# One more second-order Strassen product, with its sums in the buffer of the exchanged activations

## The chip, the cores and the metric

The kernel runs on one core of one Trainium2 chip. A core has TensorE (PE in the profile; its weight loads are listed as PEld), VectorE (DVE), ScalarE (ACT), GpSimd (POOL) and SyncE (SP), which issues most of the DMAs. The metric is the device time of one execution in microseconds (us), lower is better.

## The reference

The input `x` has the shape (8, 4096, 192). A causal convolution of 7 taps runs along the sequence, with a softmaxed set of 7 weights for each of 8 heads of 24 channels; then a two-layer network with a hard-swish gate follows on 32768 tokens.

```python
w = softmax(weight, axis=-1)                       # (8 heads, 7 taps)
y = sum over k of w[head, k] * x_pad[:, t + k, :]  # (8, 4096, 192)
h = y.reshape(32768, 192) @ w_in                   # (32768, 2048)
g = h * clip(h + 3, 0, 6) / 6
out = g @ w_out                                    # (32768, 192), float32
```

## The kernel before

**Blocks.** The tokens are worked off in 32 blocks of 1024 (`TB`), each as two halves of 512 (`N`). Block 0 is handled apart, with the preparation of the weights. Blocks 1 to 31 each run `first_layer(i, jobs)` and then `second_layer(i, between)`. All instructions stand in a fixed order written by hand (`manual_schedule`): each engine works off its own list in that order, and the framework puts in the semaphores.

**First layer (line 496).** The 2048 hidden channels of both token halves are 16 groups, `n` = 0 to 15, each of two PSUM banks. `begin(n)` multiplies the high and low parts of `w_in` and `y`, ScalarE scales the sum by 4097 in place (line 520), and `end(n)` adds the mixed part; then ScalarE makes the ReLU (`relu`, line 302) and VectorE the gate (`gate`, line 306) into `g`. There are four slots of two banks; `begin(n + 4)` needs the slot that `gate(n)` frees. Groups 0 to 7 read `y_own`, groups 8 to 15 read `y_other`, the same activations with the two halves of the partitions exchanged by six DMAs (`swap_parts`, line 490, on SP's queue). In between come the `jobs`: VectorE finishes the previous block's output (`finish`), and makes taps of the convolution of the next block (line 921, one instruction for 128 x 1536 elements). After each odd group GpSimd works too: for n = 1, 3, 5, 7 four sums of 128 x 256 (`small_sums`, line 578) into the tile `s1`, and for n = 9, 11, 13 a sum of 128 x 1024 (`g_sums`, line 412) into `S3`; for n = 9 and 11 it also issues an adding DMA (line 557) that makes `S1 = A21 + A22` in place. The rest of `S1` is added by VectorE at the layer's end (line 559).

**The tiles.** `s1` and the output tile `results` share one buffer (tag "shared"), so the first write to `s1` comes after the last store DMA out of `results`.

**Second layer (line 589).** `g` is split into four quarters A11, A21, A12, A22, and the product with `w_out` is made by Strassen's seven products, P1 to P7. TensorE runs four streams side by side, each on 32 of its columns, and writes 32 PSUM partitions each. Streams 0, 1, 2 hold the three groups of 32 output columns (`q` = 0, 1, 2); stream 3 takes what is made by Strassen once more, with seven small products of half the tokens (`small`, `level_two`): two thirds of P1 and two thirds of P5. A stream has a clock in steps; a matmul on 512 tokens costs two steps, one on 256 tokens one step. Each stream comes out at 82 steps. Everything else is put between the matmuls with `do(t, ...)` at step `t - 0.5`, and the whole is sorted by step, so that `t` sets the order on each engine's list and no waiting time. Small products need sums of their operand: those of P1 are GpSimd's, those of P5 (`s5`, in A22) are made by VectorE at steps 16.2 to 34.5, and `g_sums` makes S2 and S3 from step 38 on (product 6 reads S2 from step 46 on, product 3 reads S3 from step 66 on, and both are collected in the bank `b`).

Of the kernel before, what the change touches and what calls it, by code (L numbers as in the profile page):

```python
# [25 lines left out]
def kernel(  # L26
# [16 lines left out]
    N = 512  # L43
# [76 lines left out]
    w_s = cst.tile([P, 2, 4, NP // 2, QS], F32, name="w_s")  # L120
# [375 lines left out]
    def first_layer(i, jobs):  # L496
# [44 lines left out]
        for n in range(count):  # L541
# [11 lines left out]
            if n > NP and n % 2:  # L553
                pair = slice(n - NP - 1, n - NP + 1)
                g_sums(nc.gpsimd if n + 1 < count else nc.vector, (3,), range(NP)[pair], 2)
                if n + 3 < count:
                    nc.gpsimd.dma_start(out=S1[:, pair], in_=A22[:, pair], accum_op=ALU.add)
        for pair in (slice(NP - 2, NP), slice(NP - 4, NP - 2)):
            add(S1[:, pair], A21[:, pair], A22[:, pair])
# [29 lines left out]
    def second_layer(i, between):  # L589
        last = i + 1 == NB  # L590
        ours = [free_slots.pop(0) for _ in range(3)]
        d, e, b, x_, a, c = (psum[:, 2 * n + k] for n in ours for k in range(2))
        ends = [psum[:, 2 * free_slots[0] + k] for k in range(2)] if last else [b, b]
# [6 lines left out]
        A, E = e[rows(3)], a[rows(3)]  # L600
        first, second, third, fourth = (rows(q) for q in range(4))
# [27 lines left out]
        def small(n, m_, out, start=False):  # L629

            x, w = prod[n]
            sums, ws = (s1[-1], w_s[:, 0]) if n == 1 else (s5, w_s[:, 1])
# [10 lines left out]
            for u in range(NP // 2):  # L643
                put(3, 1, lambda u=u: matmul(
                    3, out[:, lo], wm[:, u], xm[:, u], start and u == 0
# [10 lines left out]
        def tiles():  # L656
# [3 lines left out]
            late.update(zip(("p7", "p5", "u3"), (results[0][m, n] for n in range(3))))  # L660

        for q in range(NQ):
            plain(q, d, 4, q, every, True)
            before = (1, 6, NP)[q]
            plain(q, c, 7, q, every[:before], True)
            plain(q, e, 1, 2, range(5 + q, 6 + q))
            do(clock[q], copy, out=e[rows(q + 1)] if q < 2 else p1[third], in_=e[rows(q)])
            plain(q, c, 7, q, every[before:])
            plain(q, a, 2, q, every[:6], True)
            plain(q, b, 6, q, every)  # L670
            plain(q, a, 2, q, every[6:])
# [42 lines left out]
        level_two(1, lambda: p1, range(5), "1 x5 6 5 2 7 3 4")  # L714
        do(14, copy, out=e[first], in_=V)
# [7 lines left out]
        for t, n in ((16.2, 1), (16.2, 2), (30.5, 3), (34.5, 4)):  # L723
            do(t, small_sums, s5, S1, (n,), nc.vector)
        do(32, tiles)
        do(34, lambda: copy(out=late["p7"], in_=c[m]))
        do(38, copy, out=b[m], in_=p1[:])
        do(38, g_sums, nc.vector, (2,), every, 4)
        do(38, g_sums, nc.vector, (4,), every, 4)
# [289 lines left out]
```

## Time and profile before

| | before |
|---|---|
| median of 3 timed runs | 2228.0 us (2227.92 to 2228.14) |
| span of the profiled execution, first to last instruction | 2224.9 us |
| PE busy | 2218.0 us, 100% of the span |
| DVE busy | 1894.3 us, 85% |
| ACT busy | 1379.2 us, 62% |
| POOL busy | 823.8 us, 37% |
| granted TensorE clock | 0.999 |

The profiled execution has no other time on record than its span; the median of the timed runs lies 3.1 us above it, which is what lies around the first and the last instruction. Durations in the profile are those of one execution. Matmuls overlap on TensorE, so a PE that is busy for 100% is not at its peak; the start-to-start distance of its instructions tells more.

### The profile page before, as it was taken

To read this page: it belongs to the slowest core of one execution; us is meant where nothing else is said; L and a number is where in the kernel's file an instruction comes from. 1 tells how busy PE (TensorE), PEld (TensorE's weight loads), DVE (VectorE), ACT (ScalarE), POOL (GpSimd) and SP (SyncE) were. 2 spreads that over 40 slices of the span, in tenths; PEclk is the share of its full clock that TensorE was granted. 3 is DMA by queue.
4 is the path that set the end of the run, shared out by engine and by line. 5 is a ranking of instruction groups with operands and counts; after the bars stand their busy time and mean duration, and the time that the engine had idled before them with its cause. 6 is when DMAs were issued, how large, how long until landed. Compare 5 with 4: busy or idle time off the path is not lost.

```text
span 2224.9 us, 50339 instructions
## 1 busy us (share of the span) xinstructions
PE 2218.0 (100%) x21496; PEld 1532.7 (69%) x21496; DVE 1894.3 (85%) x1673; ACT 1379.2 (62%) x1678; POOL 823.8 (37%) x690
## 2 busy tenths in 40 slices
PE   9999999999999999999999999999999999999999
PEld 5467776677766777766777667776677776677766
DVE  8888888888888888888888888888888888888876
ACT  7457665576655676555766557665567655576654
POOL 2344432344422444223443234442244422344323
PEclk9999999999999999999999999999999999999999
DMA  6244224443244342344422444324434234442232
GB/s 157 57 98 85 49 58 91 85 83 62 53 82 91 77 80 47 71 91 84 85 48 58 91 87 81 67 49 82 91 79 81 47 67 91 84 84 52 55 77 34
DMA packets 253584, 166.57 MB, mean 75 GB/s; under 512 B 208017, under 2 KB 213137, under 8 KB 253361
## 3 DMA queue, kind: packets, MB, share of 16 engines
q1 hardware_dynamic: 234872, 129.46, 28.4%
q0 software_dynamic: 17248, 33.64, 8.7%
q8 instruction: 168, 2.75, 0.5%
q14 instruction: 56, 0.45, 0.1%
q10 hardware_dynamic: 1240, 0.27, 0.1%
HBM read 31.72 MB, written 25.17 MB: 26 GB/s over the span
## 4 chain that ended last, share of the span: by engine, by line
PE 99%; DVE 0%; DMA 0%; ACTq 0%; issue 0%; DVEq 0%; ACT 0%
PE psum L615 49%; PE psum L508 46%; PE psum L296 2%; PE psum L341 2%; DMA x<-in_x_dram 0%; DVE y L255 0%; DVE top L175 0%; ACTq L89 0%; PE psum L816 0%; DVE results L456 0%; DVE scale L171 0%; DVE y L251 0%; DVE scale L192 0%; DVEq L1014 0%; DVE results L462 0%
## 5 line engine op out<-in xcount | busy, mean ns | idle before, releaser
L615 PE MATMUL psum<-g,w_out 128*32 128x512 f32 (+1 forms) x6712 | 967.5, 552 | 0.0
L306 DVE SCALAR_TENSOR_TENSOR g<-g,psum 128x1024 f32<-128x1024 f32 (+1 forms) x528 | 618.3, 1186 | 198.8 <-ACT g L302 194.5
L578 POOL TENSOR_TENSOR s<-g 128x256 f32<-128x256 f32 x248 | 273.6, 1103 | 1241.1 <-DVE g L306 1200.5
L302 ACT ACTIVATE g<-psum,half 128x1024 f32<-128x1024 f32 (+1 forms) x528 | 564.8, 1087 | 6.0 <-PE psum L508 5.2
L615 PEld LDWEIGHTS psum<-g,w_out 128*32 128x32 f32 x6712 | 371.8, 110 | 246.0 <-issue 126.7
L508 PE MATMUL psum<-y,w_in 64*128 64x512 f32 x4464 | 521.4, 388 | 0.0
L508 PE MATMUL psum<-y_other,w_in 64*128 64x512 f32 x4464 | 516.0, 386 | 0.0
L520 ACT ACTIVATE psum<-psum 128x1024 f32<-128x1024 f32 x465 | 469.0, 1008 | 50.7 <-PE psum L508 48.4
L508 PEld LDWEIGHTS psum<-y,w_in 64*128 64x128 f32 x4464 | 413.5, 184 | 115.7 <-issue 26.0
L508 PEld LDWEIGHTS psum<-y_other,w_in 64*128 64x128 f32 x4464 | 418.1, 184 | 87.8
L615 PE MATMUL psum<-s,w_out 128*32 128x512 f32 (+1 forms) x3272 | 465.5, 570 | 0.0
L921 DVE SCALAR_TENSOR_TENSOR y<-x,c_sb,y 128x1536 f32<-128x1536 f32 x186 | 335.2, 1802 | 2.6 <-ACT y L919 1.3
L412 POOL TENSOR_TENSOR s<-g 128x1024 f32<-128x1024 f32 x93 | 285.9, 3074 | 26.2 <-DVE g L306 26.2
L615 PE MATMUL psum<-g,w_s 128*32 128x256 f32 x1240 | 282.8, 379 | 0.0
L615 PEld LDWEIGHTS psum<-s,w_out 128*32 128x32 f32 x3272 | 154.3, 110 | 81.9 <-issue 49.4
L615 PEld LDWEIGHTS psum<-g,w_s 128*32 128x32 f32 x1240 | 136.4, 110 | 67.7
L412 DVE TENSOR_TENSOR s<-g 128x2048 f32<-128x2048 f32 (+1 forms) x93 | 181.3, 1977 | 1.1
L615 PE MATMUL psum<-s,w_s 128*32 128x256 f32 x744 | 170.7, 379 | 0.0
L578 DVE TENSOR_TENSOR g<-g 128x1024 f32<-128x1024 f32 x124 | 151.7, 1224 | 5.3
L412 DVE TENSOR_TENSOR g<-g 128x2048 f32<-128x2048 f32 x62 | 139.1, 2284 | 0.0
L612 ACT COPY psum<-psum 32x512 f32<-32x512 f32 x93 | 51.3, 551 | 135.4 <-PE psum L615 135.4
L456 DVE TENSOR_TENSOR results<-psum,results 32x256 f32<-32x256 f32 (+3 forms) x128 | 69.3, 541 | 50.9 <-issue 45.5
(91 smaller groups left out, 1299.5 us busy)
## 6 DMA issues: line engine op xcount, KB each, us to landing
y_other<-y SPq DMA_DIRECT2D x186, 384.0 KB, 5.1
g<-g POOLq DMA_DIRECT2D x62, 512.0 KB, 5.0
out_dram<-results SPq DMA_DIRECT2D x378, 64.0 KB, 2.0
x<-in_x_dram SPq DMA_DIRECT2D x53, 388.5 KB, 7.7
stage<-in_moe_w_in_dram SPq DMA_DIRECT2D x16, 192.0 KB, 4.5
stage<-in_moe_w_out_dram SPq DMA_DIRECT2D x8, 384.0 KB, 6.8
x<-in_x_dram SPq DMA_DIRECT2D x7, 384.0 KB, 8.4
x<-in_x_dram POOLq DMA_DIRECT2D x2, 388.5 KB, 5.4
```

What stands on the lines that cost most here:

```text
L296: nc.tensor.matmul(out=psum[:, b], lhsT=w[r], rhs=src, start=start, stop=stop, skip_group_check=onto,)
L302: nc.scalar.activation(r6, h, ACT.Relu, bias=half[:], scale=1.0 / 6.0)
L306: nc.vector.scalar_tensor_tensor(out=g_, in0=g_, scalar=1.0, in1=h, op0=ALU.min, op1=ALU.mult)
L341: lambda p=p: nc.tensor.matmul(out=bank[j * QS : (j + 1) * QS, tokens], lhsT=w_out[:, p, w, cols], rhs=x[:, p, tokens], start=(first and p ...
L412: engine.tensor_tensor(out=o[:, r], in0=a[:, r], in1=b[:, r], op=op)
L456: nc.vector.tensor_tensor(out=out, in0=x, in1=y, op=op)
L508: nc.tensor.matmul(out=psum[:, 2 * slots[n] + k], lhsT=r32(w_in_parts[part][r, c, s]), rhs=r32(y_other[0][r, part, s] if group else y_own[ ...
L520: nc.scalar.mul(both(n), both(n), 4097.0)
L578: engine.tensor_tensor(out=o, in0=p, in1=q, op=op)
L612: streams[3].append((t - 0.5, lambda: fn(*args, **kw)))
L615: nc.tensor.matmul(out=out, lhsT=w, rhs=x, start=start, stop=True, tile_position=(0, j * QS), skip_group_check=True,)
L921: jobs.append(lambda k=k: nc.vector.scalar_tensor_tensor(out=y[:], in0=x[:, :, k : k + N], scalar=c_sb[:, k : k + 1], in1=y[:], op0=ALU.mu ...
```

## The change

- P2's first two thirds (`q` = 0, 1) are made by Strassen once more, too: seven small products on streams 0 and 1 in place of 16 matmuls on 512 tokens. P1's remaining third is cut into half matmuls over all four streams. Every stream then comes out at 81 steps in place of 82.
- The four sums of A12 that P2's small products need (`sums2`) are made by VectorE at the start of the second layer. They stand, with `p1`, in a new tile `z2` with the tag of `y_other`, hence in the same buffer; a third set of small weights is made once, in block 0's stage.
- Since `z2` occupies that buffer until P2 is added up (step 65.6), `swap_parts` moves from step 18 to step 70.
- All four parts of `S1` are added by DMA from GpSimd's queue; VectorE's two additions of 128 x 1024 go. Two of the four s5 sums move behind S2, to step 40, and the sums for S3 are cut in two.
- The convolution's taps are cut into three instructions of 128 x 512 each. None stands in the second layer any more; 18 of them, instead of four taps of 128 x 1536, stand in the first layer: four behind `finish`, and then 1, 2, 1, 2, 1, 2, 1, 1, 1, 1, 1 after groups 0 to 10.
- P2 is collected in `late["p2"]` by four copies and three additions on 32 or 96 partitions.

```diff
-    w_s = cst.tile([P, 2, 4, NP // 2, QS], F32, name="w_s")
+    w_s = cst.tile([P, 3, 4, NP // 2, QS], F32, name="w_s")
...
                 g_sums(nc.gpsimd if n + 1 < count else nc.vector, (3,), range(NP)[pair], 2)
-                if n + 3 < count:
-                    nc.gpsimd.dma_start(out=S1[:, pair], in_=A22[:, pair], accum_op=ALU.add)
-        for pair in (slice(NP - 2, NP), slice(NP - 4, NP - 2)):
-            add(S1[:, pair], A21[:, pair], A22[:, pair])
+                nc.gpsimd.dma_start(out=S1[:, pair], in_=A22[:, pair], accum_op=ALU.add)
...
+        z = pools[0].tile([P, NP + 1, N], F32, name="z2", tag="other")
+        sums2, p1 = z[:, 0:NP], z[0:DH, NP]
...
+        A2, B2, C2, E2 = a[rows(0)], a[rows(1)], x_[rows(0)], x_[rows(1)]
...
+        def by_half(j, bank, n, q, ch, t, start=False):
+            x, w = prod[n]
+            put(j, 1, lambda: matmul(
+                j, bank[rows(j), halves[t]], w_out[:, ch, w, q * QS : (q + 1) * QS],
+                x[:, ch, halves[t]], start,
+            ))
...
+        def after(j, fn, *args, **kw):
+            do(clock[j], fn, *args, **kw)
...
         for q in range(NQ):
             plain(q, d, 4, q, every, True)
-            before = (1, 6, NP)[q]
+            before = (0, 2, 6)[q]
             plain(q, c, 7, q, every[:before], True)
-            plain(q, e, 1, 2, range(5 + q, 6 + q))
-            do(clock[q], copy, out=e[rows(q + 1)] if q < 2 else p1[third], in_=e[rows(q)])
-            plain(q, c, 7, q, every[before:])
-            plain(q, a, 2, q, every[:6], True)
+            if q == 0:
+                by_half(0, e, 1, 2, 7, 0)
+            elif q == 1:
+                by_half(1, e, 1, 2, 4, 1)
+                plain(1, e, 1, 2, (5, 6))
+            else:
+                by_half(2, e, 1, 2, 7, 1)
+            after(q, copy, out=e[rows(q + 1)] if q < 2 else p1[third], in_=e[rows(q)])
+            if q == 0:
+                small(2, 1, A2, True, 0)
+                after(0, copy, out=B2[:, lo], in_=A2[:, lo])
+            elif q == 1:
+                small(2, 6, B2, False, 1)
+                after(1, copy, out=C2[:, lo], in_=B2[:, lo])
+            plain(q, c, 7, q, every[before:], before == 0)
+            if q == 0:
+                small(2, 7, C2, False, 0)
+                small(2, 2, A2, False, 0)
...
+            elif q == 1:
+                small(2, 5, E2, True, 1)
...
+            else:
+                plain(2, a, 2, 2, every[:6], True)
+            assert clock[q] == 45
             plain(q, b, 6, q, every)
-            plain(q, a, 2, q, every[6:])
+            if q == 0:
+                small(2, 4, C2, False, 0)
+            elif q == 1:
+                small(2, 3, B2, False, 1)
+            else:
+                plain(2, a, 2, 2, every[6:])
...
-        for t, n in ((16.2, 1), (16.2, 2), (30.5, 3), (34.5, 4)):
-            do(t, small_sums, s5, S1, (n,), nc.vector)
...
+        do(0, small_sums, sums2, A12, (1, 2, 3, 4), nc.vector)
+        do(26, small_sums, s5, S1, (1, 2), nc.vector)
...
         do(38, g_sums, nc.vector, (2,), every, 4)
-        do(38, g_sums, nc.vector, (4,), every, 4)
-        do(62, lambda: add(late["u3"], b[m], late["p7"]))
+        do(40, small_sums, s5, S1, (3, 4), nc.vector)
+        do(41.2, lambda: copy(out=late["p7"], in_=c[m]))
+        do(46, g_sums, nc.vector, (4,), range(0, 4), 4)
+        do(61.2, lambda: add(late["u3"], b[m], late["p7"]))
+        do(61.4, g_sums, nc.vector, (4,), range(4, 8), 4)
...
+        do(65.6, lambda: add(late["p2"], late["p2"], p1))
+        do(65.6, lambda: store(i, late["p2"], 0, 0))
...
-        def conv_jobs(i):
+        def conv_jobs(i, width=1):
...
             for k in range(1, KC):
...
+                for s in range(0, K3, width):
+                    jobs.append(lambda k=k, s=s: tap(k, slice(s, s + width)))
...
-            jobs = {4 * n + 1: [job] for n, job in enumerate(conv[4:])}
-            jobs[-1] = left + conv[3:4]
+            jobs = {-1: left + conv[:4]}
+            pieces = conv[4:]
+            for n, k in enumerate((1, 2, 1, 2, 1, 2, 1, 1, 1, 1, 1)):
+                jobs[n], pieces = pieces[:k], pieces[k:]
...
-                between = [(13, split_high), (15, split_rest), (18, swap_parts)]
+                between = [(13, split_high), (15, split_rest), (70, swap_parts)]
             if i + 2 < NB:
-                between += [(20, begin_conv), (60, lambda: conv[0]()), (72, lambda: conv[1]()), (73, lambda: conv[2]())]
+                between += [(20, begin_conv), (60, lambda: conv.pop(0)())]
```

## The prediction

> **What bounds the kernel now.** First the page's chain of waits, then the chain in order of time, then a table of the two stages of one block (1057.14 to 1090.05 us first layer, 1090.05 to 1125.51 second).
>
> ```profile
> PE 99%; DVE 0%; DMA 0%; ACTq 0%; issue 0%; DVEq 0%; ACT 0%
> PE psum L615 49%; PE psum L508 46%; PE psum L296 2%; PE psum L341 2%; DMA x<-in_x_dram 0%; DVE y L255 0%; DVE top L175 0%; ACTq L89 0%; PE psum L816 0%; DVE results L456 0%; DVE scale L171 0%; DVE y L251 0%; DVE scale L192 0%; DVEq L1014 0%; DVE results L462 0%
> ```
>
> ```profile
> 1057.14 32.90 PE psum L508 x288
> 1090.05 35.47 PE psum L615 x216
> ```
>
> ```profile
> core 0: us, PE busy (x) PEld busy (x) DVE busy (x) ACT busy (x) POOL busy (x), PEclk, DMA share, GB/s
> 1057.14:1090.05 32.91, 32.91 (x293) 26.84 (x296) 25.94 (x23) 30.83 (x32) 21.99 (x19) 1.00 0.16 26
> 1090.05:1125.51 35.46, 35.46 (x386) 21.15 (x386) 33.09 (x27) 11.82 (x20) 3.67 (x2) 1.00 0.59 120
> ```
>
> TensorE is the chain, at full clock: a block takes 68.37 us, and 31 such blocks are 2119 of the 2225 us. Nothing that the change does to another engine can gain time; it can only make TensorE wait. So I need how near the others are to that: VectorE has 7.0 us free in the first layer and 2.4 in the second. Its list at a block's start, and GpSimd's beside it:
>
> ```profile
> 1057.79 0.69 DVE L456 TENSOR_TENSOR results<-results 96x512 f32<-96x512 f32 x1 [1.11 <-ACT results L772]
> ...
> 1060.47 1.77 DVE L921 SCALAR_TENSOR_TENSOR y<-x,c_sb,y 128x1536 f32<-128x1536 f32 x1
> 1062.38 1.22 DVE L306 SCALAR_TENSOR_TENSOR g<-g,psum 128x1024 f32<-128x1024 f32 x1
> 1064.32 1.22 DVE L306 SCALAR_TENSOR_TENSOR g<-g,psum 128x1024 f32<-128x1024 f32 x1 [0.72 <-ACT g L302]
> 1065.46 1.81 DVE L921 SCALAR_TENSOR_TENSOR y<-x,c_sb,y 128x1536 f32<-128x1536 f32 x1
> 1067.19 2.39 DVE L306 SCALAR_TENSOR_TENSOR g<-g,psum 128x1024 f32<-128x1024 f32 x2
> 1070.39 1.22 DVE L306 SCALAR_TENSOR_TENSOR g<-g,psum 128x1024 f32<-128x1024 f32 x1 [0.82 <-ACT g L302]
> ```
>
> ```profile
> 1065.62 2.25 POOL L578 TENSOR_TENSOR s<-g 128x256 f32<-128x256 f32 x1 [40.32 <-DVE g L306]
> 1067.95 0.75 POOL L578 TENSOR_TENSOR s<-s,g 128x256 f32<-128x256 f32 x1
> 1068.65 0.74 POOL L578 TENSOR_TENSOR s<-g 128x256 f32<-128x256 f32 x1
> ```
>
> Gates come every 2.04 us. GpSimd's first sum takes 2.25 us in place of 0.74: it started inside the tap of 1065.46 and ended 0.6 after it, so a tap holds GpSimd up. The reverse, from block 0's stage:
>
> ```profile
> 9.01 2.46 DVE L255 SCALAR_TENSOR_TENSOR y<-x,c_sb,y 128x256 f32<-128x256 f32 x6
> 17.24 3.20 DVE L255 SCALAR_TENSOR_TENSOR y<-x,c_sb,y 128x256 f32<-128x256 f32 x6
> ```
>
> ```profile
> 16.86 1.32 POOL L200 TENSOR_TENSOR w_in<-sig,scale 128x384 f32<-128x384 f32 x1 [3.21 <-DVE sig L196]
> ```
>
> The same six taps take 0.74 more when GpSimd runs a sum as they start. Gates (one operand in PSUM) show no such loss at 1068 to 1072.
>
> **The change part by part.**
>
> *TensorE's steps.* 82 steps take 35.47 us, 0.4326 each; one step less is -0.43 a block. 16 matmuls on 512 tokens become 28 on 256, each of two passes: 24 passes more. Start to start, a round of four passes takes 0.4293 and one of five 0.4317, so 24 x 0.0024 = +0.06. Together -0.37, in 31 blocks **-11.5 us**. The streams now stand half a matmul apart in steps 13 to 29; the trace has no such rounds. Bounds: nothing, or an uncovered weight load (0.11, PEld row) in 16 rounds, 1.8 a block; I take nothing, by the rounds of five. The Trainium skill (TensorEngine Tiling (Array Packing), Instruction Overhead) gives every matmul some 60 cycles of overhead; as an estimate, 25 ns at the full clock, 24 passes would cost 0.6 a block and the step's gain would be gone. The rounds of five speak against it: their fifth pass cost 2.4 ns.
>
> *Taps in the first layer.* Start to start a tap of 256 elements takes 0.396 us and one of 1536 takes 1.73, so one of 512 takes 0.66. `finish` ends at 1060.47 as before. Four taps: gate 0 starts at 1063.12 in place of 1062.38, 0.74 late. A gate takes 1.14 to the next instruction, so gate and one tap 1.80, gate and two taps 2.46, against 2.04. Lateness of gates 0 to 6: 0.74, 0.60, 1.03, 0.83, 1.25, 1.01, 1.43; after that it falls by 0.24 a gate. The slack: `begin(8)` needs gate 4, which ends naturally at 1071.61; 138 matmuls of 32.90 / 288 us stand before `begin(8)`, which puts it at 1072.90, and its weights load one pair (0.23) ahead: 1.06 less the semaphore, say 1.04. So TensorE waits 1.43 - 1.04 = **0.39** a block.
>
> *GpSimd against these taps.* `s1` waits for the last store out of `results`. SP issues in order, and the exchange now stands ahead of the six stores of `finish`. VectorE's list from step 61 on (p5 0.44, u3 0.72, half of S3 2.20, p7 0.72 and 0.64, two adds 0.88, P2 0.72 and 0.64) ends 1.4 us before the layer does; then three stores at 0.5; so the exchange starts at the layer's end. It moves 2.36 MB; at the 220 GB/s of its busy slices that is 10.7 us, with the 2 of latency 12.7; the stores land behind it at about 15 us into the first layer. GpSimd starts there, where it started at 8.5, and has no pause left. From then on its 0.7-us sums stand in a row while 8 taps come: where the two take turns, the tap behind gate 4 waits for half a sum (0.3), and between the two behind gate 5 a whole one gets in (0.45 net). That is at gate 6, the latest one, so it counts in full: **0.75**. Bounds: 0 (GpSimd yields), and 1.9 (each tap waits).
>
> *The second layer.* P2's sums cost VectorE 4.7 us (four of 1.14 to 1.32) before S2; the two adds for S1 (2.28) and two s5 sums (2.4) go or move behind it. From gate 15's end to S2's first half: 15.6 before (1093.4 to 1109.0), 15.6 after, but wanted at step 45, one earlier: 0.5 of slack becomes 0.1. GpSimd's remaining work, 16 x 0.70 + 8 x 0.5 of waiting + three sums of 2.45 and two DMA issues of 1.0, ends at 15 + 24.6 = 39.6 us, while VectorE wants to start its own 128 x 1024 sum at about 37.5; before, that sum already waited 0.5. So S2 comes 0 to 2.0 late and with it product 6; I take **1.0**. The adding DMAs for the last parts of S1 are issued by about 42 and need 5.0 (page); VectorE reads S1 first at 47 or later, so they just hide, and if they don't, S2 pays for it one for one. Six more small copies on ScalarE (0.34 to 0.58 each) fall into its 23.6 us of idle time. Queued on SP behind the moved exchange are only `finish`'s stores, counted above; the load of `x` goes ahead of it.
>
> *Sum.* 30 x (0.39 + 0.75 + 1.0) = 64.2 (the last block has no taps), less 11.5: +53. On the profile: 2224.9 + 53 = 2278, and with the 3.1 around it **2281 us**.
>
> **Rivals.**
> *The step comes through* (faster): all lateness stays within the slack. VectorE has 7.0 us free in the first layer, and the taps add only 18 x 0.66 - 4 x 1.77 = 4.8. It decides if gate 6 is under 1.04 late: taps 0.06 shorter would do, if GpSimd cost nothing as well. 2228 - 11.5 = 2216. Against: the taps stand at the front, and the 7 us lie at the end too. Chance 0.17.
> *GpSimd yields*: only the late gates count: 30 x 0.39 - 11.5, 2228. Chance 0.08.
> *More collisions*: every tap waits (1.9) and the three 2.45-us sums hold VectorE's sums for the full 2.0: 30 x 4.3 - 11.5 = 117, 2345; from 2320 on I count it here. Chance 0.10.
> *The exchange comes too late*: `begin(8)` reads it 15.7 us into the layer; I have it landed at 12.7. If it takes over 3 us longer (a landing of 8.2 in place of 5.1 is the longest seen), the rest is a wait: 2 us would give 31 x 2, 2343 in all. Chance 0.03.
> *The passes' overhead* (that page's rule): +0.6 a block from odd rounds, 31 x 0.6 = 19 more, 2300. Against: the 2.4 ns. Chance 0.02.
>
> **How the numbers follow.** The forecast has 0.60. Its own range is 2245 to 2320. The range 2222 to 2330 leaves out the first rival and the far end of the third. Faster by over 0.2% (4.5 us, about what a measurement can tell here) is the first rival, 0.17; within, the second, 0.08; slower, the rest, 0.75.
>
> **What would show it.** Right: L508's stretch grows from 32.9 to about 34, with weight loads waiting for gates near groups 8 to 10; taps longer than 0.75 beside GpSimd's sums; the first sum into `s` waiting for a store and starting near 15 us; L615's stretch at 36 in place of 35.1, with a wait for S2. Wrong: a first layer of 32.9, or taps of 0.74 throughout.

## The result and the profile after

| | before | after |
|---|---|---|
| median of the timed runs | 2228.0 us (2227.91 to 2228.22) | 2545.1 us (2543.3 to 2556.4) |
| span of the profiled execution | 2224.9 us | 2542.6 us |
| granted TensorE clock, mean | 0.999 | 0.978 |
| first layer / second layer, mean of the blocks | 32.91 / 35.47 us | 33.65 / 45.19 us |

The change makes the kernel slower by 317 us: the ratio is 1.1435, 95% interval 1.1418 to 1.1452. I had forecast 2281. The sign was right; the size was far outside the range. The layers' lengths are worked out from the trace, from the first matmul of one layer to the first of the next.

The chain of waits of the page, by engine and by line, was TensorE for 99% before. Now:

```profile
PE 37%; DVE 24%; POOL 18%; DMA 8%; issue 7%; ACT 3%; SPq 2%; DVEq 0%; POOLq 0%; ACTq 0%
PE psum L615 29%; POOL s L575 12%; PE psum L508 8%; DVE y L973 8%; DMA g<-g 6%; POOL s L412 6%; DVE g L306 6%; DVE results L456 4%; DVE s L412 3%; DMA out_dram<-results 2%; SPq L372 2%; DVE g L575 2%; ACT g L302 1%; POOL g L556 1%; DVE y L9
```

One block's first and second layer, in the table of stretches:

```profile
core 0: us, PE busy (x) PEld busy (x) DVE busy (x) ACT busy (x) POOL busy (x), PEclk, DMA share, GB/s
1121.53:1155.43 33.90, 33.50 (x290) 26.55 (x289) 31.37 (x37) 30.77 (x32) 18.22 (x19) 1.00 0.48 101
1155.43:1198.15 42.72, 39.02 (x414) 19.05 (x412) 34.57 (x30) 14.24 (x26) 8.83 (x6) 1.00 0.36 61
```

In the second layer TensorE is idle for 3.7 us and busy for 39.0, where 35.1 was wanted: after a wait the four streams are out of step, and for some 4.3 us only one or two of them run (an estimate from the starts of the matmuls, with 0.43 us for one on 512 tokens and 0.21 for one on 256). How a block comes to that, as the chain in order of time tells it (start, length, what; 1121.53 is the block's start):

```profile
1131.41 0.96 SPq L372
1132.42 3.79 DMA out_dram<-results
...
1136.60 0.74 POOL s L575
...
1159.59 2.87 POOL s L412
...
1162.78 0.70 POOL g L556
1163.48 7.12 DMA g<-g
1170.72 1.24 DVE g L575
...
1173.31 0.44 DVE z L456
1173.79 3.65 PE psum L615 x26
```

The last store of `finish` is behind the exchange and lands 14.7 us into the block; GpSimd starts then, ends at 41, issues the last adding DMA, and this lands at 49.1. VectorE's first two s5 sums (L575, two of 1.2) start then, and P1's additions (L456) stand behind them. But VectorE had waited only 0.28 for the landing: its own list had come to these sums just before, at 48.9. In the whole execution its idle time ahead of them comes to 21.7 us put down to this DMA, 0.7 a block:

```profile
L575 DVE TENSOR_TENSOR g<-g 128x1024 f32<-128x1024 f32 x124 | 148.9, 1222 | 25.0 <-DMA g<-g 21.7
```

So two chains arrive together, GpSimd's with its DMA and VectorE's own list, and the chain of waits shows only the one that comes last. P1's last small product cannot start until its bank has been read: TensorE's wait there is 2.98 us. Waits of TensorE are given from the start of the last matmul ahead of the wait to the start of the next one; the time for which the profile calls it idle is some 0.4 to 0.6 shorter. Two more follow, 0.81 (step 41, behind a copy into the same bank) and 1.47 (step 67, behind the addition of P7 and P4, which stands on VectorE behind half of S3).

Why GpSimd is late, and VectorE too, is in the two lists. First GpSimd's (start, length), then VectorE's:

```profile
1145.53 0.74 POOL L575 TENSOR_TENSOR s<-s,g 128x256 f32<-128x256 f32 x1
1146.23 1.19 POOL L575 TENSOR_TENSOR s<-g 128x256 f32<-128x256 f32 x1
...
1159.59 2.87 POOL L412 TENSOR_TENSOR s<-g 128x1024 f32<-128x1024 f32 x1
```

```profile
1145.90 0.91 DVE L973 SCALAR_TENSOR_TENSOR y<-x,c_sb,y 128x512 f32<-128x512 f32 x1
1146.74 1.21 DVE L306 SCALAR_TENSOR_TENSOR g<-g,psum 128x1024 f32<-128x1024 f32 x1
...
1158.91 1.22 DVE L412 TENSOR_TENSOR s<-g 128x1024 f32<-128x1024 f32 x1
1160.06 3.50 DVE L575 TENSOR_TENSOR z<-g 128x1024 f32<-128x1024 f32 x1
...
1168.67 1.75 DVE L477 SCALAR_TENSOR_TENSOR y<-y,y 128x1536 fp32r<-128x1536 f32 x1
...
1170.72 2.56 DVE L575 TENSOR_TENSOR g<-g 128x1024 f32<-128x1024 f32 x2 [0.28 <-DMA g<-g]
1173.31 0.98 DVE L456 TENSOR_TENSOR z<-psum,z 32x256 f32<-32x256 f32 x2
```

A tap that falls into GpSimd's sums makes one of them 1.19 long in place of 0.74, while the tap itself, start to next start, takes 0.84 in place of 0.67. And VectorE's first sum for P2 starts at 1160.06, 0.47 after the start of a GpSimd sum that ends at 1162.46: if it waits for that end, its 3.50 are 2.40 of waiting and its own 1.1. From the sum behind gate 15 (1158.91) to P1's addition (1173.31) VectorE takes 14.4 us, against 9.9 in the kernel before: four sums for P2, some 4.5 by themselves, stand where two additions for S1 took 2.3, and the rest is almost all that waiting.

About half of the blocks are worse than this one (second layers of 46 to 48 in place of 42 to 44), and the first layer tells them apart. In 14 blocks VectorE gives way, as here: its taps lose about 1.1 us in all, the first layer takes 33.9 and the second 42.4 to 44.1. In 15 blocks GpSimd gives way: the taps keep their pace, five of GpSimd's sums of 128 x 256 take 1.7 to 2.5, the first layer takes only 33.3, and the second 46.1 to 48.1. The first block (40.4) stands apart. The two kinds differ in when GpSimd's first sum starts: at 14.8 to 15.2 us of the block where VectorE gives way, at 14.1 to 14.7 (once 15.5) where GpSimd does. Whether that decides it was not tested.

In the next block, one of the second kind, VectorE takes 17.9 us from the sum behind gate 15 to P1's addition, of which it waits 1.0 for the DMA. The wait at step 33 is 5.68 us, and the clock is cut (the same table, slices of 1 us around that wait):

```profile
1250.00:1251.00 1.00, 0.00 (x0) 0.00 (x0) 0.72 (x1) 0.00 (x0) 0.00 (x0) 1.00 0.00 0
1251.00:1252.00 1.00, 0.00 (x0) 0.00 (x0) 0.90 (x2) 0.00 (x0) 0.00 (x0) 0.64 0.00 0
...
1254.00:1255.00 1.00, 1.00 (x9) 0.35 (x2) 0.00 (x0) 0.00 (x0) 0.00 (x0) 0.50 0.00 0
...
1258.00:1259.00 1.00, 1.00 (x12) 0.50 (x6) 1.00 (x1) 0.00 (x0) 0.00 (x0) 0.95 0.00 0
```

TensorE's last matmul ended at 1248.3 and the next began at 1253.35. The granted clock (the number behind the bracket of POOL) halves 3.0 us into this silence and stays at 0.50 until 1258.1, 4.8 us after the work has begun again. From there to the wait at step 41 TensorE takes 6.4 us, and 4.1 in the block above, which had no cut: so the cut costs 2.3 on top of the wait. The length of a silence alone does not decide it. Of the 29 silences of over 1.5 us in this trace, from the end of one matmul to the start of the next, the two of 2.4 us left the clock alone, five of the eleven of 2.8 to 2.9 were followed by a cut, and so were all sixteen of 3.3 to 5.8. Each cut lasted 3.4 or 6.8 us, began 2.2 to 4.9 us after the last matmul, and ended 2.7 to 6.0 us after work had begun again. All in all 88 us of such work ran at half clock, which is worth at most 44 of the 317 us (an estimate from the trace's clock records). The Trainium skill (TensorE: Matmul & The Clock Gate, Part 1) says that the clock is halved after some 3.4 us without work and given back after as much sustained work. The trace agrees in size only: here a silence of 2.8 us can be enough.

### The profile page after: what moved, and what is told of

Its sections match the earlier page's. It is cut to its first block, busy times and chain, and to the rows that moved or that the text cites. A ratio compares the mean times of both kernels' runs of the same rounds, so it can differ in the third digit from the quotient of the medians.

```text
span 2542.6 us, 53029 instructions
## 1 busy us (share of the span) xinstructions
PE 2366.6 (93%) x22364; PEld 1486.7 (58%) x22364; DVE 2149.4 (85%) x2157; ACT 1452.9 (57%) x1864; POOL 918.7 (36%) x756
## 3 DMA queue, kind: packets, MB, share of 16 engines
q0 software_dynamic: 34112, 66.14, 15.2%
## 4 chain that ended last, share of the span: by engine, by line
PE 37%; DVE 24%; POOL 18%; DMA 8%; issue 7%; ACT 3%; SPq 2%; DVEq 0%; POOLq 0%; ACTq 0%
PE psum L615 29%; POOL s L575 12%; PE psum L508 8%; DVE y L973 8%; DMA g<-g 6%; POOL s L412 6%; DVE g L306 6%; DVE results L456 4%; DVE s L412 3%; DMA out_dram<-results 2%; SPq L372 2%; DVE g L575 2%; ACT g L302 1%; POOL g L556 1%; DVE y L993 1%
## 5 line engine op out<-in xcount | busy, mean ns | idle before, releaser
L615 PE MATMUL psum<-g,w_out 128*32 128x512 f32 (+1 forms) x6340 | 1058.3, 536 | 0.2 <-ACT psum L612 0.2
L575 POOL TENSOR_TENSOR s<-g 128x256 f32<-128x256 f32 x248 | 268.6, 1083 | 1473.8 <-DVE y L973 736.9
L615 PE MATMUL psum<-s,w_out 128*32 128x512 f32 (+1 forms) x3272 | 631.2, 592 | 0.0
L615 PE MATMUL psum<-g,w_s 128*32 128x256 f32 x1488 | 350.9, 406 | 141.3 <-DVE z L456 116.6
L973 DVE SCALAR_TENSOR_TENSOR y<-x,c_sb,y 128x512 f32<-128x512 f32 (+1 forms) x546 | 416.9, 790 | 1.5 <-ACT y L971 1.4
L412 POOL TENSOR_TENSOR s<-g 128x1024 f32<-128x1024 f32 x93 | 251.0, 2699 | 2.8 <-DVE g L306 2.7
L412 DVE TENSOR_TENSOR s<-g 128x2048 f32<-128x2048 f32 (+1 forms) x93 | 248.7, 2674 | 2.0
L615 PE MATMUL psum<-z,w_s 128*32 128x256 f32 x744 | 203.2, 422 | 20.7 <-ACT psum L738 13.4
L615 PEld LDWEIGHTS psum<-s,w_out 128*32 128x32 f32 x3272 | 175.9, 110 | 52.0 <-ACT psum L612 7.1
L612 ACT COPY psum<-psum 32x256 f32<-32x256 f32 x186 | 82.7, 445 | 212.4 <-PE psum L615 209.5
L456 DVE TENSOR_TENSOR results<-psum,results 32x256 f32<-32x256 f32 (+1 forms) x190 | 96.1, 506 | 115.3 <-PE psum L615 99.6
L575 DVE TENSOR_TENSOR g<-g 128x1024 f32<-128x1024 f32 x124 | 148.9, 1222 | 25.0 <-DMA g<-g 21.7
```

What stands on the lines that cost most here:

```text
L412: engine.tensor_tensor(out=o[:, r], in0=a[:, r], in1=b[:, r], op=op)
L456: nc.vector.tensor_tensor(out=out, in0=x, in1=y, op=op)
L575: engine.tensor_tensor(out=o, in0=p, in1=q, op=op)
L612: streams[3].append((t - 0.5, lambda: fn(*args, **kw)))
L615: nc.tensor.matmul(out=out, lhsT=w, rhs=x, start=start, stop=True, tile_position=(0, j * QS), skip_group_check=True,)
L973: nc.vector.scalar_tensor_tensor(out=y[:, r], in0=x[:, r, k : k + N], scalar=c_sb[:, k : k + 1], in1=y[:, r], op0=ALU.mult, op1=ALU.add,)
```

## The experiments

Three theories. **G**: GpSimd is held up by the short taps and starts late, and what it owes comes late. **V**: VectorE's list of the second layer has the wrong order, and what TensorE needs stands behind what waits. **D**: the landing of S1's last part by DMA is the loss, however the rest is arranged. The layers' lengths are means of the blocks. Where no interval is given, a kernel was run once; the five executions of the changed kernel lie within 13 us of each other, those of the kernel before and of the last one within 2.

| kernel | first / second layer | us | against before |
|---|---|---|---|
| before | 32.91 / 35.47 | 2227 | |
| + short taps | 33.27 / 37.70 | 2305 | +78 |
| + exchange at step 70 | 33.07 / 36.32 | 2257 | +30 |
| + S1 all by DMA | 32.92 / 48.64 | 2624 | +397 |
| + S1 by DMA, exchange | 33.02 / 38.95 | 2337 | +110 |
| + all three | 33.29 / 43.92 | 2493 | +265 |
| after (P2 on top) | 33.65 / 45.19 | 2545 | +317 |

Where S1 is all by DMA, the first two s5 sums stand at step 26, as in the change (16.2 before).

**Parts of the change, each put into the kernel before.** The taps:

```diff
-            jobs = {4 * n + 1: [job] for n, job in enumerate(conv[4:])}
-            jobs[-1] = left + conv[3:4]
+            jobs = {-1: left + conv[:4]}
...
+            for n, k in enumerate((1, 2, 1, 2, 1, 2, 1, 1, 1, 1, 1)):
```

> The kernel before with only the convolution's taps cut into 128 x 512 and moved into the first layer, as in the change. Theory G (GpSimd falls behind in the first layer, by the late start of its sums and by taking turns with VectorE's taps, and hands S1 over late): L508's stretch grows by 0.4 us (gates late) plus 0.3 to 0.8 (collisions), L615's stays within 0.5 of 35.47, so 2228 + 30 x 0.7 to 1.5 = 2249 to 2273 us. Theory V (the waits come from the order of VectorE's list in the second layer, which stands unchanged here): only the late gates count, 2228 to 2242 us.

Measured 2305, beyond both theories. The first layer grows by 0.36 (0.28 in most blocks), the second by 2.2, though not one instruction of it was changed. GpSimd's list and VectorE's, then VectorE's list of the kernel before at the same place:

```profile
1059.86 2.86 POOL L412 TENSOR_TENSOR s<-g 128x1024 f32<-128x1024 f32 x1
```

```profile
1057.77 2.13 DVE L412 TENSOR_TENSOR s<-g 128x1024 f32<-128x1024 f32 x1
1059.94 5.01 DVE L456 TENSOR_TENSOR g<-g 128x1024 f32<-128x1024 f32 x2
...
1070.80 0.43 DVE L456 TENSOR_TENSOR p<-psum,p 32x256 f32<-32x256 f32 x1
```

```profile
1093.45 1.71 DVE L412 TENSOR_TENSOR s<-g 128x1024 f32<-128x1024 f32 x1
...
1103.39 0.43 DVE L456 TENSOR_TENSOR p<-psum,p 32x256 f32<-32x256 f32 x1
```

From the sum after gate 15 to P1's addition VectorE took 9.9 us before, with no idle time between, and TensorE had no wait for the addition: the matmul behind it began 0.84 after its end. Now GpSimd's last sum runs in the same place, the same stretch takes 13.0, and TensorE waits 1.94 for P1's addition. So of 3.1 us 0.8 were slack, and the rest is the second layer's growth. G and V are two halves of one thing: GpSimd's lateness reaches TensorE through VectorE's list, here without any adding DMA on the way.

The exchange:

```diff
-                between = [(13, split_high), (15, split_rest), (18, swap_parts)]
+                between = [(13, split_high), (15, split_rest), (70, swap_parts)]
```

> The kernel before with only the exchange of y moved from step 18 to step 70. Theory G: the stores of finish land some 7 us later, GpSimd's first sum starts near 14 us into the first layer in place of 8.5, its last 128 x 1024 sum ends some 4 us later and VectorE's own sum and additions at the layer's end wait for it: 1 to 2.5 us a block, 2259 to 2305 us. Theory V: GpSimd may start late but nothing in the chain waits for it, 2228 to 2235 us.

Measured 2257, just under G's range: GpSimd's first sum starts at 13.5 us of the block in place of 8.5, its last ends at 38.7 (36.9).

S1 all by adding DMA:

```diff
-                if n + 3 < count:
-                    nc.gpsimd.dma_start(out=S1[:, pair], in_=A22[:, pair], accum_op=ALU.add)
-        for pair in (slice(NP - 2, NP), slice(NP - 4, NP - 2)):
-            add(S1[:, pair], A21[:, pair], A22[:, pair])
+                nc.gpsimd.dma_start(out=S1[:, pair], in_=A22[:, pair], accum_op=ALU.add)
```

> The kernel before with one part of the change: all four pairs of S1 added by DMA, and the s5 sums 1 and 2 at step 26 as in the change (16.2 before). Nothing else is altered: 82 steps, whole taps, the exchange at step 18. Theory D: GpSimd's last sum ends at 36.9 us of the block, the DMA is issued by 39 and lands 7 to 8 later, 13 to 14 us into the second layer, where step 26 is at 11.2: the s5 sums wait 2 to 3 us with P1's additions behind them, TensorE loses 1 to 3 us a block, time 2260 to 2320. Theory V: here VectorE has no sums for P2, is freed of two additions (2.3 us), and nothing is lost: 2224 to 2240.

Measured 2624, worse than the whole change, and far beyond both theories. The chain in order of time, and the table of stretches over the wait:

```profile
1277.78 17.34 DMA g<-g
...
1298.31 23.07 PE psum L612 x125
```

```profile
1287.00:1298.30 11.30, 0.99 (x10) 0.08 (x3) 2.89 (x4) 1.16 (x2) 0.00 (x0) 0.75 0.91 197
1298.30:1321.00 22.70, 22.69 (x218) 11.64 (x218) 19.50 (x16) 4.32 (x8) 0.00 (x0) 0.90 0.12 19
```

The adding DMA takes 17.3 us where the changed kernel's takes 7.1, because the exchange goes out at step 18 just as it is issued: the DMA engines are busy for 0.91 of the wait. VectorE waits 14.8 us for it, TensorE 10.9 behind VectorE, and then it runs at a mean clock of 0.90.

Both together (S1 as above, exchange at 70):

> The kernel before with two parts of the change together: S1 all by adding DMA (s5 sums 1 and 2 at step 26, as in the change) and the exchange at step 70. With S1 by DMA alone the last adding DMA, issued as the exchange runs, took 17.3 us to land and the time was 2624; with the exchange at 70 alone it was 2257. Theory D' (an adding DMA and the exchange in flight together hold each other up, so the two parts belong together): the landing falls to 7 to 8.4, the s5 sums wait 2 to 4 us past their place, time 2290 to 2370. Theory D (the adding DMA is slow by itself): 2500 or more.

Measured 2337, as D' has it; the last adding DMA of the block at 963.77 landed in 6.6 us. So the two edits belong together: moving the exchange costs 30 by itself and saves 287 once S1 is added by DMA. All three, without P2's second level:

> The kernel before (82 steps, P2 plain) with the change's three other parts together: taps cut and moved, the exchange at step 70, S1 all by adding DMA with s5 1 and 2 at step 26. Without the taps' part it was 2337. Theory G (short taps hold GpSimd up, and every microsecond of that goes through the adding DMA into the s5 sums): 2420 to 2490, and P2's second level with its four sums and its list accounts for the remaining 55 to 125 of the change's time. Theory V (most of the loss is P2's own, VectorE's list): 2345 to 2375, and P2 accounts for 170 or more.

Measured 2493: G, 3 us above its range. 265 of the change's 317 us come with the three edits that touch no TensorE step. The other 52 are not simply the price of P2's second level. In this kernel VectorE stands idle for 146 us in all, 4.9 a block, for the adding DMA; in the change P2's four sums fill most of that time (21.7 us are left). And here GpSimd gives way in 25 of 30 blocks, in the change in 15. Among blocks of the same kind P2 adds 2.5 us to the second layer where GpSimd gives way (44.9 to 47.4) and 3.8 where VectorE does (39.3 to 43.1).

**Parts of the change undone.** S1's last two pairs by VectorE again:

```diff
+                if n + 3 < count:
...
+        for pair in (slice(NP - 2, NP), slice(NP - 4, NP - 2)):
+            add(S1[:, pair], A21[:, pair], A22[:, pair])
```

> The changed kernel with the last two pairs of S1 added by VectorE at the end of the first layer, as in the kernel before; all else as changed. Theory D (S1's last landing by DMA, 7 to 8.4 us behind GpSimd's end, holds the s5 sums): the landing is gone, the s5 sums start 2.5 to 3.5 us earlier, time 2435 to 2470. Theory V (VectorE is too full at the layer's start): the two additions (2.3 to 5 us beside GpSimd) now stand ahead of the four sums for P2, TensorE waits for these at step 13 or so, and the gain is eaten: 2510 or more.

Measured 2597 (33.58 / 47.02), 52 worse than the change, as V has it. The edit takes the landing away but puts two additions onto VectorE ahead of P1's, so it does not by itself measure what the landing costs; that D is not the sole cause rests on VectorE's 0.7 a block above and on the taps alone, which lose without it. Without the landing, VectorE's own list is the chain (the chain in order of time of one block):

```profile
1183.51 4.31 DVE s L412
...
1188.98 1.22 DVE g L456
...
1200.71 0.44 DVE z L456
1201.19 5.00 PE psum L618 x26
```

The taps whole and at their old places:

> The changed kernel with the taps whole (1536 elements) and where they were in the kernel before; all else as changed. Theory G (GpSimd loses its turns to the short taps, ends at 41 to 44 us of the block in place of 37, and the last adding DMA and the s5 sums with it come 2 to 6 us later): the L615 stretch falls by 3 to 5 us, time 2390 to 2450. Theory V (the order of VectorE's list decides, whenever GpSimd ends): only the first layer gains its 0.7, 2520 to 2530.

Measured 2463 (33.06 / 43.06), 82 better, between the two theories. The second layer falls by 2.1, less than G says, to what the better half of the changed kernel's blocks have: the last adding DMA still takes 7.2 behind GpSimd's end, and VectorE's first sum for P2 still meets a GpSimd sum (4.07).

The exchange from GpSimd's queue in place of SP's:

```diff
-        nc.sync.dma_start(out=to[D2:P], in_=part[0:D2])
+        dma.dma_start(out=to[D2:P], in_=part[0:D2])
```

> The changed kernel with the exchange issued from GpSimd's queue in place of SP's, so that the stores of finish don't stand behind it. Theory G: GpSimd's first sum starts near 9 us into the first layer in place of 14 to 15, the last adding DMA lands some 5 us earlier, and a block loses 4 to 5 of its 10 us of waits: 2390 to 2430 us. Theory V: VectorE still waits in the same places, 2480 us or more.

Measured 2582, in V's range, but it decides nothing, since what the edit was to bring did not come: SP's stores no longer stand behind the exchange in a queue, but they are still late (GpSimd's first sum at 13.7 us), and GpSimd has six issues more.

**The order of VectorE's list.** Only the places at which the s5 sums and the addition of P7 and P4 stand:

```diff
-        do(26, small_sums, s5, S1, (1, 2), nc.vector)
+        do(29.2, small_sums, s5, S1, (1, 2), nc.vector)
...
-        do(62, lambda: add(late["p7"], late["u3"], d[m]))
+        do(61.3, lambda: add(late["p7"], late["u3"], d[m]))
```

> The changed kernel with two moves in VectorE's list alone: the first two s5 sums go from step 26 to 29.2, behind the first addition to p1, and P7's second addition from step 62 to 61.3, ahead of the second half of S3. Theory V: the wait of TensorE before step 33 (3.0 us in one block) and the one before P5's fourth small product (1.5 us) go, 2545 - 31 x 4 = 2420 us or less. Theory G: S1 still comes late, and product 6 waits for S2 in place of step 33; only the 1.5 us go, 2480 to 2510 us.

Measured 2470 (33.39 / 42.93), 75 better and just better than G's range; V's 2420 is not reached. With the sums at 33.2, behind both of P1's additions:

> The changed kernel with two places of its list altered, no work more or less: the s5 sums 1 and 2 stand at step 33.2 (26 in the change), behind both additions of P1 in place of ahead of them, and the addition of P7 and P4 at 61.3 (62). Theory V (what TensorE loses in the second layer, it loses to additions that stand on VectorE behind the s5 sums, which wait for the adding DMA): both of P1's additions now run before the wait, the L615 stretch falls from 45.2 to 38 or less, time at most 2330. Theory D (the late landing itself is the loss, because S2 and product 6 stand behind the s5 sums wherever these are put): the wait only moves, to product 6 or the second group of P5; L615 at 41 or more, time 2415 or more. With the s5 sums at 29.2, between the two additions, it was 2470 and 42.9.

Measured 2471 (33.38 / 42.96), where theory D put it, but not for D's reason. The adding DMA is gone from the chain (VectorE's idle time for it is 5.3 us in all), but the list before it is not shorter: gate 15, a sum of 4.45 and one of 3.98 beside GpSimd, three more for P2, the two operations that split y. TensorE's gaps only move (1.97 at step 24, 2.10 at 33, 2.23 at 49). Then the whole list in due order (the lines that these replace, and the two halves of `split_rest` as functions, are left out):

```diff
-                between = [(13, split_high), (15, split_rest), (70, swap_parts)]
+                between = [(13, split_high), (24, split_low), (29.1, split_mix), (70, swap_parts)]
...
+        do(33.2, small_sums, s5, S1, (1,), nc.vector)
+        do(38, g_sums, nc.vector, (2,), range(0, 4), 4)
+        do(38.1, small_sums, s5, S1, (2,), nc.vector)
+        do(38.2, g_sums, nc.vector, (2,), range(4, 8), 4)
+        do(45.6, small_sums, s5, S1, (3, 4), nc.vector)
```

> The changed kernel with VectorE's list of the second layer put in the order in which TensorE wants its parts, no work more or less: the split of the next block's y (two operations of 1.75) goes from step 15 to 24 and 29.1, each behind what is due before it; the s5 sums at 33.2, 38.1 and 45.6, between them the halves of S2; the addition of P7 and P4 at 61.3. Theory V (order): VectorE is then never behind by itself, the L615 stretch falls below 38, time 2320 or less. Theory G (VectorE is late because its own first sums run beside GpSimd's 2.4 to 2.9 us sums and take 4 in place of 1.2, and because GpSimd ends late): the list still starts some 5 us late, the stretch is 39.5 to 41.5, time 2370 to 2430.

Measured 2394 (33.40 / 40.46): G, so order alone does not do it. Upon that, whole taps (one at step 74, one ahead of gate 0, one behind each of gates 1, 3, 5, 7):

> As the run before (list in due order), and the taps whole: one at step 74, one ahead of gate 0, and one behind each of gates 1, 3, 5 and 7. Theory G: GpSimd, no longer cut off by short taps, ends 2 to 3 us earlier, but its last sum still runs beside VectorE's first ones: the stretch is 37 to 39.5, time 2290 to 2370. Theory V: no more than the first layer's 0.5, within 20 us of the run before.

Measured 2312 (33.14 / 37.98): G again. Upon that, the sum behind gate 13 on VectorE:

```diff
+                if n + 3 == count:
+                    held = pair
+                    continue
+                for pair in ([held] if n + 1 == count else []) + [pair]:
```

> As the run before (due order, whole taps), and the sum into S3 behind gate 13 made by VectorE behind gate 15 in place of GpSimd, so that GpSimd has done when VectorE's own sums start. Theory G: the sums take 1.2 again, the last adding DMA is issued some 3 us earlier, VectorE meets every step, and the 81 steps come through: L615 35.1 to 36, L508 33.0, time 2215 to 2250. Theory D (the landing of S1's last part holds the s5 sums however early it is issued): the stretch stays above 37, time 2290 or more.

Measured 2295 (33.13 / 37.42), which is D's range, but VectorE's idle time for the adding DMA is 0.6 us in the whole execution. VectorE's first sums take no more than 1.58 now, but the steps do not come through: the trace shows no wait of TensorE over 0.81 us in the block, and 2.3 us lost in small ones.

**Whether small waits add up.** Four of those waits mended by moving single operations:

```diff
-                    do(clock[3], steps[k])
+                    do(45.1 if (n, k) == (5, 1) else clock[3], steps[k])
...
-        do(38.2, g_sums, nc.vector, (2,), range(4, 8), 4)
+        do(45.1, g_sums, nc.vector, (2,), range(4, 8), 4)
...
-        do(61.2, lambda: add(late["u3"], b[m], late["p7"]))
+        do(60.9, lambda: add(late["u3"], b[m], late["p7"]))
...
-                between = [(13, split_high), (24, split_low), (29.1, split_mix), (70, swap_parts)]
+                between = [(4.6, split_high), (24, split_low), (29.1, split_mix), (70, swap_parts)]
```

> The kernel of c3_n13 with the four waits mended that its trace still shows, no work more or less: the copy of A to B in P5 goes from step 41 to 45.1 (TensorE's start of P2's fifth part stood 0.81 behind it, same bank), P2's addition ahead of the second half of S2 (0.4 at step 49), the addition of U3 ahead of P5's addition (0.8 at step 65, of which half), and the split on ScalarE from 13 to 4.6 (0.27 at step 20). Theory of single waits (they add up): L615 falls from 37.4 by 1.9 to about 35.5, time 2230 to 2242. Theory of a further bound (VectorE's list as a whole is the limit): the waits move, 36.5 or more, 2265 or more.

Measured 2304 (33.25 / 37.62), a miss: the moved copy now stands right ahead of P5's second part, which needs it, and TensorE waits 1.64 there in place of 0.81. The other three are smaller or gone. The exchange early (with c5_waits as the start):

```diff
-        do(61.4, g_sums, nc.vector, (4,), range(4, 8), 4)
...
+        do(65.6, g_sums, nc.vector, (4,), range(4, 8), 4)
...
+                between = [(4.6, split_high), (24, split_low), (29.1, split_mix), (65.7, swap_parts)]
```

> As c5_waits, and P2 ended ahead of the second half of S4, so that the exchange goes out some 4 us earlier (step 65.7, ahead of P2's stores). Theory G: s1 starts 3 to 5 us earlier, GpSimd ends earlier, the last landing too; what is left of the late sums goes, 2222 to 2235. Rival: with an earlier start GpSimd meets one or two more whole taps, the first layer grows by 0.3 to 0.6, and nothing waits for GpSimd's end any more: 2238 to 2255.

Measured 2341 (33.39 / 38.60), above both: the second half of S3, now behind P2's additions, is 1.37 late for product 3, which neither theory had. One more chunk of P5 between the copy and its reader, again from c5_waits:

```diff
-            "1 l4 2 6 5 7 3 l2 4 l2 h8" if last else "1 x2 2 6 5 7 3 x1 4 x5",
+            "1 l4 2 6 5 7 3 l2 4 l2 h8" if last else "1 x3 2 6 5 7 3 4 x5",
```

> As c5_waits, with one more chunk of P5 between its first and second part (three in place of two), so that the moved copy of A has two steps before A is written again. Theory of single waits: the 1.64 at step 45 goes, L615 35.7 to 36.1, time 2240 to 2255. Theory of a further bound: 37 or more, 2280 or more.

Measured 2361 (33.39 / 39.36), in the range of a further bound. The wait ahead of P5's second part fell to 0.79, but the later parts of P5 now meet reads of their banks: 1.52 at step 61 and 0.81 at step 65. And P1 in another order, with one copy out of its bank later:

```diff
-        level_two(1, lambda: p1, (), "6 5 2 7 3 4")
+        level_two(1, lambda: p1, (), "6 5 7 3 2 4")
...
-            after(q, copy, out=e[rows(q + 1)] if q < 2 else p1[third], in_=e[rows(q)])
+            do(clock[q] if q < 2 else 33.1, copy, out=e[rows(q + 1)] if q < 2 else p1[third], in_=e[rows(q)])
```

> As c7_order5, and in P1 the parts in the order 6 5 7 3 2 4 (6 5 2 7 3 4), so that part 3 no longer starts behind a copy into its bank (0.4 at step 29). Theory of single waits: L615 35.2 to 35.7; with a first layer of 33.2 this is 68.6 a block against 68.4 before, time 2224 to 2242: no gain is left, since what the step saves (0.37) goes into gates that are late behind the taps (0.3). Theory of a further bound: 2270 or more.

Measured 2344.6, ratio 1.0524 (1.0506 to 1.0541), second layer 38.81, again in the range of a further bound. The 0.4 at step 29 is gone as expected (the two moves were not made one by one), the other two stand. The reads that they meet, moved behind:

```diff
-                    do(45.1 if (n, k) == (5, 1) else clock[3], steps[k])
+                    do(44.9 if (n, k) == (5, 1) else clock[3], steps[k])
...
-        do(61.3, lambda: add(late["p7"], late["u3"], d[m]))
+        do(63.2, lambda: add(late["p7"], late["u3"], d[m]))
+        do(63.2, g_sums, nc.vector, (4,), range(4, 8), 4)
...
-        do(65.4, lambda: copy(out=p2(first, hi), in_=C2[:, lo]))
+        do(67.1, lambda: copy(out=p2(first, hi), in_=C2[:, lo]))
```

> As c8_order1, with the addition of P7 and P4 behind P5's part 7 (step 63.2 in place of 61.3, the second half of S4 behind it), the copy of P2's last quarter behind P5's part 3 (67.1 in place of 65.4), and the copy of P5's A ahead of P2's two at step 45. Theory of single waits: the second layer, 38.8 in c8, loses the 1.52, the 0.81 and 0.3 to 0.6, 35.9 to 36.2; with 33.3 to 33.4 for the first layer the time is 2252 to 2264, still above before by the gates that are late and by waits under 0.3. Theory of a further bound: 37.2 or more, 2290 or more.

Measured 2256.5 (2256.2 to 2257.3), ratio 1.0135 (1.0118 to 1.0152), 33.04 / 36.23: single waits, and they add up. Its chain of waits, by engine, and the rest of the loss in one block, in order of time:

```profile
PE 88%; DVE 7%; DMA 2%; ACT 1%; issue 1%; SPq 0%; POOL 0%; DVEq 0%; ACTq 0%; POOLq 0%
```

```profile
1052.76 1.22 DVE g L579
...
1054.45 2.31 DVE g L412
...
1056.80 12.45 PE psum L619 x92
```

With the same 81 steps and the same arithmetic, 289 of the 317 us are given back by where things stand, by whole taps, and by one sum that went from GpSimd to VectorE. What is left is VectorE, some 0.4 late with each half of S2 (the lines above are the second half), some smaller waits, and 0.13 in the first layer. No version here beats the kernel before.

## Why the prediction was wrong

- **TensorE's steps (-0.37 a block): right as far as it can be seen.** In the last kernel the first 44 steps, 18 of P2's small matmuls among them, take 19.10 us, 0.434 a step against 0.4326 before: a surplus of 0.06. The whole layer has 28 passes more by the profile's rows (414 against 386), where the sum counted 24; 20 of them lie in these steps. At the 25 ns that the prediction took from the Trainium skill (TensorEngine Tiling (Array Packing), Instruction Overhead), 20 passes would cost 0.5, as an estimate. That does not show here.
- **Late gates (0.39): about right.** With the taps alone the first layer grew by 0.36 in the mean and by 0.28 in most blocks. In the change it is some 0.43 where the taps lose nothing.
- **GpSimd against the taps (0.75, bounds 0 and 1.9): the collision was there, but in half of the blocks its bill went to the other engine.** Where VectorE gives way its taps lose about 1.1, and the first layer is 0.6 longer than where GpSimd does. Where GpSimd gives way, its five slow sums push its end to 43.1 us of the block in place of 40.7, and the second layer is 4.3 longer. So the rival "GpSimd yields" had its condition fulfilled in 15 blocks, and they are the slow ones, not the 2228 that it gave.
- **The start of s1 at about 15: right** (15.1). GpSimd's end, 39.6 in the sum, came at 41 to 43: its three large sums take 2.4, 2.9 and 2.9.
- **The second layer (1.0, bounds 0 and 2.0): this is the step that failed; it measured 10.1** (45.19 against the 35.1 of 81 steps). Three faults in it. First, the wrong reader. "15.6 before, 15.6 after" follows VectorE's list to S2, and "S2 pays one for one" prices lateness there. But P1's additions stand in that list ahead of S2, and TensorE waits for them at step 33. Up to them the trade is not even: P2's four sums come in ahead, and the two s5 sums that go away had stood behind the first of them. That stretch grew from 9.9 to 14.4 us, and to 17.9 in a block of the slower kind, where before only 0.84 was free. Second, GpSimd's last sums were to hold VectorE's up by 2.0 at most; they cost it 2.4 in the one block and about 5 in the other. The adding DMA, issued at 41.2, took 7.1 and not 5.0 to land; since VectorE's list came to S1 at 48.9 and not at 47, it was late by 0.28 only, 0.7 in the mean, so "they just hide" was nearly right, and by luck: both were 2 us late. Third, one for one was wrong by itself: streams out of step then meet their banks' reads (0.81, 1.47) and run by ones and twos, and the clock is cut behind most of the long waits.
- **The rivals** had the right mechanisms at wrong sizes. "More collisions" put a cap of 2.0 on the second layer; the range ended at 2330 for that reason alone.

## What to carry to other kernels

When work is put into an in-order list, or one of its operations starts to wait for a transfer or for another engine, price everything that is queued behind it, at the first consumer that runs dry, and not at the one that you had in mind. An engine that is 93% busy in a stage may have hardly any slack up to a certain operation (here 0.84 us): follow the list to each reader. When two engines get into each other's way, price both outcomes, since either may give way. Where two chains arrive together, the chain of waits names only the later one; how long the engine itself was idle shows what the wait is worth. A wait of about 3 us or more can cost TensorE more than its length, and a schedule with many tight places is repaired in the order of the trace, one wait at a time, since each move makes new neighbours.

## What the runs showed of the hardware that I had not expected

- Two engines that share turns do not lose alike, and not always the same way. GpSimd's 128x256 sum goes from 0.74 to 1.19 beside taps of 512 elements, which go from 0.67 to 0.84; or it goes to 1.7 to 2.5, and the taps keep their 0.67. Beside a whole tap (1.77) a sum takes 2.1 to 2.3, and some taps 2.0 to 2.4. The Trainium skill (SBUF — State Buffer, Who interferes with whom) says that a VectorE instruction with two inputs in SBUF contends with a GpSimd instruction that reads SBUF, and that the order of issue decides who waits; the first sum for P2, whose 3.50 are the 2.40 that were left of GpSimd's sum and its own 1.1, agrees.
- The same adding DMA took 5.1 to 8.6 us in this place without the exchange in flight, and 15.7 to 18.5 beside it in all blocks but one.
- TensorE's clock was cut behind all silences of 3.3 us and more and behind five of eleven of 2.8 to 2.9, each time for 3.4 or 6.8 us, much of it after the work had begun again.
- TensorE also waits for a copy that touches other partitions of its bank: the wait of 0.81 at step 41 is for a copy into the fourth quarter of a bank (partitions 96 to 127) into whose second quarter P2's small product goes. The semaphores are the framework's. The Trainium skill (PSUM — Partial Sum Buffer, PSUM bank collisions raise a hardware error) says that accesses in different quarters may go on at once; whether these waits could be left out was not tried.
